# Closing the framework's context behind the first load, and a third direct block at the end

## The chip, the cores and the metric

The kernel runs on one core of one Trainium2 chip. The metric is device time of one launch in microseconds (us); lower is better. The core has TensorE (PE, with its weight loads as PEld), VectorE (DVE), ScalarE (ACT), GpSimd (POOL) and SyncE (SP, which here only issues transfers), and 16 DMA engines that all transfers share.

## What is computed

One decode step: a gated sum of an attention block over a long cache and an MLP block, for two rows `x` of 1024 numbers, all in float32.

```
g = sigmoid((x * gate_w).sum(-1, keepdims=True))
a = _A_ref(x, A_k_cache, A_v_cache, A_wq, A_wo)   # 32 query heads, 4 kv heads, 32768 keys
b = _B_ref(x, B_w1, B_w2, B_w3, B_w4)
return g * a + (1 - g) * b
...
x1 = x + hs            # S = 1: the shifted hs is 0, so w1 and w2 drop out
h2 = _gelu(_layernorm(x1, axis=-1) @ w3) @ w4
return x1 + h2
```

The cache and the weights, 331 MB, are read once. There are two rows of x and each number of the cache meets few numbers of the other operand, so nearly all of the work is the reading.

## The kernel before

All large inputs stream through two SBUF buffers of 128 rows by 16384 columns: `buf_a` takes `wq`, the keys `kt` and `wo`, and `buf_b` takes `w3`, `w4` and the values `vt`. A load fills one buffer (8 MB, 7 MB for `w3` and `w4`); the two alternate, 19 or 20 loads each. SP issues them in one queue; each but the first two waits for a count in `go`, which DVE raises when it has taken out the results that the buffer's matmuls left. TensorE goes through the rounds of `Fori(0, ROUNDS + 1)`: in each it waits for `landed_a`, multiplies the eight sets of `buf_a`, then the eight sets of `buf_b`. A set is four matmuls of 512 columns, one for each group `g`, and each group writes its own 32 PSUM rows. Round 0 has no sets: it does the small matmuls of the start (the transposed `x` from `xg`, the sums for the norm).

The last load is the second half of `w4`. It comes in five transfers, `PIECES = (6, 4, 2, 1, 1)` slabs of 1024 columns (a slab is 512 KB and one block of 128 rows of `w4`). The first ends sets 0 to 2 and has the semaphore `landed_b`; piece 1 ends sets 3 and 4, piece 2 set 5. The last `FIN = 2` slabs are not multiplied in sets: `block(c)` multiplies each straight into the result tile `acc`, in 16 short matmuls of 128 columns (eight, each in two passes). Between the two blocks TensorE adds what DVE has folded: at the end of set 3 DVE adds one bank of `ps_b` to `acc_sb`, at the end of set 5 the other in two halves (`masked`), and each half raises `folded`. Then DVE copies `acc` to `o_sb` and SP stores it.

The program's engine code stands between `tc.tile_critical(...)` and `tc.close()`. The framework's closing, which a later line calls, makes all engines meet twice (drains and semaphore instructions, profile line L578) while POOL clears the framework's semaphores. Behind it SP waits for the store.

Of the kernel before, what the change touches and what calls it, by code (L numbers as in the profile page):

```python
# [32 lines left out]
FIN = 2  # L33
EARLY = E * KT - FIN
PIECES = (6, 4, 2, 1, 1)
# [5 lines left out]
def kernel(  # L41
# [66 lines left out]
    store = nc.alloc_semaphore("store")  # L108

    with tc.tile_critical(sync_engine=POOL, no_gpsimd_drain=True):  # L110
        new = tc.alloc_semaphore
        landed = [new("landed_a"), new("landed_b")]
        pieces = [new(f"piece{i}") for i in range(1, len(PIECES))]
        folded, fin = new("folded"), new("fin")
        ready = [new("ready_a"), new("ready_b")]
        edge, pd, dvp, acp = new("edge"), new("pe_to_dve"), new("dve_to_pe"), new("act_to_pe")
        da, ad, dp, pc, go = (new(n) for n in (
            "dve_to_act", "act_to_dve", "dve_to_pool", "pool", "dve_to_sp"))
        v, s, t, g_, sy = nc.vector, nc.scalar, nc.tensor, nc.gpsimd, nc.sync

        def take(engine, sem, n=1):
            engine.wait_ge(sem, n).then_inc(sem, -n)  # L122

        def mm(o, lhsT, rhs, start=True, stop=True):
            return t.matmul(o, lhsT, rhs, start=start, stop=stop, skip_group_check=True)  # L125


        def sets(x, which, *events):
            for n4 in which:
                for g in range(G):  # L130
                    n, bank = n4 * G + g, n4 // 2 % 2
                    last = mm(ps[x][C * g:C * g + C, bank * 512:bank * 512 + 512],
                              wt[x][:, n * C:n * C + C], buf[x][:, n * 512:n * 512 + 512],
                              n4 in (0, 2), n4 in (3, 4, 5, 7))
                if n4 in events:
                    last.then_inc(pd, 1)

        def even(k):
            return t.If(k % 2 < 1)

        with t.Fori(0, ROUNDS + 1) as k:
            with t.If(k > 0):
                with t.If(k > 1):
                    sets(1, range(6, 8), 7)
                    with even(k):
                        take(t, dvp)
                        mm(sm[:, LP:LP + REP], ones, lsel).then_inc(pd, 1)
                        take(t, dvp)
                        for e in range(E):
                            last = mm(sm[:, OP + e * REP:OP + (e + 1) * REP],  # L150
                                      pv_t[:, e * P:(e + 1) * P], sel_all)
                        last.then_inc(pd, 1)
                take(t, landed[0], 16)
                take(t, ready[0])
                sets(0, range(8), 5, 7)
                with t.If(k < ROUNDS):
                    with even(k):
                        take(t, dvp)
                        t.transpose(sm[:1, MT:MT + P], m1, ident).then_inc(pd, 1)  # L159
                        take(t, dvp)  # L160
                        mm(sm[:, BP:BP + 1], mb, ones[:1, :1]).then_inc(pd, 1)
                    for q in range(2):
                        take(t, acp)
                        for j in range(4 * q, 4 * q + 4):
                            last = t.transpose(tr[:, j * P:(j + 1) * P], p[:, j * P:(j + 1) * P], ident)  # L165
                        last.then_inc(pd, 1)
                take(t, landed[1], 16)
                take(t, ready[1])
                sets(1, range(3))
                with t.If(k > ROUNDS - 1):  # L170
                    take(t, pieces[0], 16)
                sets(1, range(3, 5), 3)
                with t.If(k > ROUNDS - 1):
                    take(t, pieces[1], 16)
                sets(1, range(5, 6), 5)
            with t.Else():
                take(t, edge, 32)
                take(t, dvp)
                for w in range(4):
                    last = mm(tr[:, :48], spread[:, w * P:(w + 1) * P],  # L180
                              x16[:, w * 48:(w + 1) * 48], w == 0, w == 3)
                last.then_inc(pd, 1)
                take(t, dvp)
                for i in range(2):
                    last = mm(sm[:, SUMS + i * B:SUMS + i * B + B], ones, part[:, i * B:i * B + B])
                last.then_inc(pd, 1)
                take(t, dvp)
                mm(sm[:, VAR:VAR + B], ones, part2).then_inc(pd, 1)

        def eighths(lhsT, rhs, start=False, stop=False, halves=range(2)):  # L190

            for h in halves:
                for g in range(G):
                    w, col = lhsT(g), rhs(g, h)
                    first = HALF * (1 - h) + w[1]
                    last = mm(acc[C * g:C * g + C], w[0][:, first:first + C], col, start and h == 0, stop and h == 1)
            return last

        def block(c):
            def columns(g, h):  # L200
                col = (EARLY + c) * D + g * (D // G) + h * P
                return buf[1][:, col:col + P]
            return eighths(lambda g: (h_fin, c * C), columns, c == 0, c == FIN - 1)

        t.wait_ge(pieces[2], 16)
        block(0)
        for h in range(2):
            t.wait_ge(folded, h + 1)
            eighths(lambda g: (sel, g // 2 * C),
                    lambda g, h: acc_sb[:, (g % 2 * 2 + h) * P:(g % 2 * 2 + h + 1) * P], halves=[h])  # L210
        t.wait_ge(pieces[3], 16)
        block(1).then_inc(fin, 1)


        x_rows = xg.rearrange("(j q) k c -> j (q k c)", j=16)
        for lo, hi in ((0, 10), (10, 16)):
            s.dma_start(x16[lo:hi], x_rows[lo:hi]).then_inc(edge, 16)
        take(s, da)
        s.activation(gate, sm[:, SUMS:SUMS + B], AF.Sigmoid).then_inc(ad, 1)
        take(s, da)  # L220
        s.activation(dev, var, AF.Sqrt).then_inc(ad, 1)
        s.wait_ge(pc, 1)
        s.sem_inc(acp, 2)

        def turn(src, bank, func, to, *dims, **kw):

            return s.activation(at(p, to, *dims, (1, H)), at(src, bank * 512, (1, 2), (P, 4), (2, H)), func, **kw)  # L227

        for src in (qs, hs):
            take(s, da)  # L230
            for d in range(2):
                last = turn(src, 0, AF.Copy, d * H, (512, 2), (P, 4))
            last.then_inc(acp, 2)
        take(s, da)
        s.activation(bent, cube, AF.Tanh, scale=math.sqrt(2.0 / math.pi)).then_inc(ad, 1)
        with s.Fori(0, PAIRS):
            for i in range(NI):
                take(s, da)
                turn((s_sb, ps[0])[i // 2], i % 2, AF.Exp, i % 2 * 512, (256, 2), (H, 4), bias=bias, scale=scale,
                     accum_out=l4[:, i:i + 1]).then_inc(acp, 1)  # L240
            s.drain().then_inc(dp, 1)


        g_.memset(ident, 0.0)
        g_.memset(spread, 0.0)
        g_.drain()
        g_.affine_select(out=ident, in_=ident, compare_op=ALU.not_equal, fill=1.0, base=0,
                         pattern=[[-1, P]], channel_multiplier=1).then_inc(pc, 1)
        for tt in (wt_ab, zeros, buf[1][:, E * F * 2:]):
            g_.memset(tt, 0.0)  # L250
        g_.drain()
        for e in range(E):
            for kk in range(2):
                for tau, (lo, hi) in enumerate(halves):
                    g_.tensor_copy(
                        at(buf[1], E * F * 2 + (e * 2 + kk) * 512 + tau * 256 + kk * P + e, (2, H), rows=(lo, hi)),
                        at(ident, lo, (1, H), rows=(lo, hi)))
        g_.drain().then_inc(pc, 1)

        def x_to_queries(load):  # L260
            g_.tensor_copy(at(wt[0], 0, (256, 4), (34, 8), (1, B)),
                           at(xs, load * 12, (3, 4), (0, 8), (1, B))).then_inc(ready[0], 1)

        def queries(m):
            for tau, (lo, hi) in enumerate(halves):
                for u in range(2):
                    for e in range(E):
                        last = g_.tensor_copy(  # L268
# [5 lines left out]
        def heads(load):  # L274
# [4 lines left out]
            last.then_inc(ready[0], 1)  # L279

        take(g_, dp)
        x_to_queries(0)
        take(g_, dp)
        x_to_queries(1)
        take(g_, dp)
# [325 lines left out]
```

## Time and profile before

| | |
|---|---|
| time, median of 3 runs | 775.51 us (775.24 to 775.61) |
| profiled execution: time | 774.93 us |
| profiled execution: span, first to last instruction | 773.2 us |
| TensorE busy / weight loads / DVE | 407.5 us / 135.6 us / 160.9 us |
| read from HBM | 331.36 MB, 429 GB/s over the span |

The time is the launch's; the span is what the profiler sees between the first and the last instruction, and 1.7 us of the profiled execution lie around it. Matmuls of the four groups overlap and the busy time of TensorE is that of their union. In a row of the timeline "x24" counts instructions; a float32 matmul is two of them.

### The profile page before, as it was taken

The page shows a single profiled execution, that of the slowest core. Times are in us where ns is not written, and L with a number is a line of the kernel's source. Part 1 is how long each engine was busy: PE and PEld are TensorE (multiplying, and loading weights), DVE is VectorE, ACT ScalarE, POOL GpSimd, SP SyncE. Part 2 cuts the span into 40 slices and gives each one's busy share as a digit, 9 for nine tenths or more (in the row PEclk, how much of TensorE's full clock was granted, in tenths as well). Part 3 has the DMA queues.
Part 4 walks back from the last instruction along what each step waited for, and adds up shares of the span by engine and source line. Part 5 has one row for each costly group of instructions (what it writes and reads, how often), then busy time and mean ns, then how long its engine had stood idle before and what let it go on. Part 6 is the DMA issues. An engine that isn't in the chain of part 4 may idle for free. (4 is left out here: it accounts for less than half of the span.)

```text
span 773.2 us, 7166 instructions
## 1 busy us (share of the span) xinstructions
PE 407.5 (53%) x2845; PEld 135.6 (18%) x2845; DVE 160.9 (21%) x384; ACT 32.2 (4%) x74; POOL 22.5 (3%) x89
## 2 busy tenths in 40 slices
PE   1555465645554545545645554545445645554547
PEld 1111121211111111111211121111111211221112
DVE  4101030203120312031203120312031203120321
ACT  1000000100010001000100010001000100010000
POOL 4001000000000000000000000000000000000000
PEclk9977777677677777677677677777677677677779
DMA  9999999999999999999999999999999999999996
GB/s 381 434 434 434 440 429 434 434 434 434 434 434 434 434 434 434 434 434 431 434 434 434 434 434 434 434 434 434 434 434 434 434 434 434 434 434 434 434 417 293
DMA packets 6404, 331.41 MB, mean 429 GB/s; under 512 B 737, under 2 KB 769, under 8 KB 1025
## 3 DMA queue, kind: packets, MB, share of 16 engines
q1 hardware_dynamic: 6368, 331.36, 99.2%
q10 hardware_dynamic: 32, 0.01, 0.0%
q8 instruction: 1, 0.02, 0.0%
q14 instruction: 3, 0.02, 0.0%
HBM read 331.36 MB, written 0.01 MB: 429 GB/s over the span
## 5 line engine op out<-in xcount | busy, mean ns | idle before, releaser
L125 PE MATMUL ps_a<-buf_a,wt_ab 128*32 128x512 f32 x1280 | 183.0, 736 | 161.9 <-PEq L122 161.9
L125 PE MATMUL ps_b<-buf_b,wt_ab 128*32 128x512 f32 x1264 | 178.6, 727 | 125.3 <-PEq L122 125.3
L125 PEld LDWEIGHTS ps_a<-buf_a,wt_ab 128*32 128x32 f32 x1280 | 50.1, 132 | 285.8 <-issue 285.8
L125 PEld LDWEIGHTS ps_b<-buf_b,wt_ab 128*32 128x32 f32 x1264 | 49.1, 131 | 243.1 <-issue 243.1
L434 DVE TENSOR_REDUCE mx<-ps_a 128x1 f32<-128x512 f32 x34 | 23.5, 692 | 267.6 <-DVEq L122 250.5
L481 DVE COPY wt_ab<-tr 64x256 f32<-64x256 f32 x128 | 53.9, 421 | 18.3 <-DVEq L122 16.5
L227 ACT ACTIVATE zeros<-s_sb,bias 128x512 f32<-128x512 f32 x16 | 12.0, 750 | 539.7 <-ACTq L122 539.7
L165 PE MATMUL tr<-ident,zeros 128*128 128x128 f32 x152 | 25.7, 315 | 14.5 <-PEq L122 13.9
L385 DVE TENSOR_TENSOR pvs<-pvs,ps_b 128x512 f32<-128x512 f32 x8 | 5.5, 688 | 108.7 <-DVEq L122 108.7
L268 POOL COPY wt_ab<-q_all 64x64 f32 x64 | 12.3, 236 | 530.3 <-POOLq L122 529.6
L390 DVE COPY pvs<-ps_b 128x512 f32<-128x512 f32 x8 | 5.5, 691 | 86.3 <-DVEq L122 86.3
L165 PEld LDWEIGHTS tr<-ident,zeros 128*128 128x128 f32 x152 | 19.1, 159 | 24.5 <-issue 24.4
L125 PE MATMUL sm<-sel_all,zeros 128*128 128x8 f32 x40 | 7.1, 286 | 29.8 <-PEq L122 29.8
L125 PEld LDWEIGHTS sm<-sel_all,zeros 128*128 128x128 f32 x40 | 6.4, 230 | 30.3 <-issue 30.3
L227 ACT ACTIVATE zeros<-ps_a,bias 128x512 f32<-128x512 f32 x16 | 11.0, 687 | 14.9 <-ACTq L122 14.9
L438 DVE COPY s_sb<-ps_a 128x1024 f32<-128x1024 f32 x9 | 10.9, 1214 | 0.0
L159 PE MATMUL sm<-ident,m 128*1 128x128 f32 x9 | 2.4, 269 | 10.1 <-PEq L122 10.1
L125 PE MATMUL tr<-x,spread 16*128 16x48 f32 x8 | 1.9, 408 | 11.0 <-PEq L122 11.0
L125 PE MATMUL sm<-ones,mb 1*128 1x1 f32 x18 | 3.6, 264 | 6.9 <-PEq L122 6.9
L395 DVE SCALAR_TENSOR_TENSOR acc_sb<-ps_b,mask_g,acc_sb 128x512 f32<-128x512 f32 (+1 forms) x5 | 3.1, 642 | 13.6 <-PE ps_b L125 13.5
L522 DVE SCALAR_TENSOR_TENSOR tmp<-pvs,mss,tmp 128x128 f32<-128x128 f32 x16 | 5.6, 351 | 1.2
L392 DVE TENSOR_TENSOR pvs<-pvs,ps_b 128x512 f32<-128x512 f32 x8 | 5.5, 687 | 0.7
(98 smaller groups left out, 102.3 us busy)
## 6 DMA issues: line engine op xcount, KB each, us to landing
buf_b<-w SPq DMA_DIRECT2D x3, 7168.0 KB, 26.6
buf_b<-w SPq DMA_DIRECT2D x1, 3072.0 KB, 17.0
buf_b<-w SPq DMA_DIRECT2D x1, 2048.0 KB, 21.5
buf_b<-w SPq DMA_DIRECT2D x1, 1024.0 KB, 23.6
buf_b<-w SPq DMA_DIRECT2D x2, 512.0 KB, 24.7
buf_a<-kt SPq DMA_DIRECT2D x16, 28.3
buf_b<-vt SPq DMA_DIRECT2D x16, 28.4
buf_a<-wq SPq DMA_DIRECT2D x2, 24.5
```

What stands on the lines that cost most here:

```text
L125: return t.matmul(o, lhsT, rhs, start=start, stop=stop, skip_group_check=True)
L165: last = t.transpose(tr[:, j * P:(j + 1) * P], p[:, j * P:(j + 1) * P], ident)
L227: return s.activation(at(p, to, *dims, (1, H)), at(src, bank * 512, (1, 2), (P, 4), (2, H)), func, **kw)
L268: last = g_.tensor_copy(at(wt[0], e * 512 + u * P + u * 16 + tau * REP, (256, 2), (C, G), (1, REP), rows=(lo, hi)), q_all[lo:hi, bass.ds(m ...
L385: v.tensor_add(dst, dst, ps[x][:, :512]).then_inc(go, 1)
L390: v.tensor_copy(dst, ps[x][:, :512]).then_inc(go, 1)
L392: return v.tensor_add(dst, dst, ps[x][:, 512:])
L395: return v.scalar_tensor_tensor(at(acc_sb, *dims), at(src, *dims), mask_g, at(acc_sb, *dims), op0=ALU.mult, op1=ALU.add)
L434: last = v.reduce_max(out=mx[:, 2 * L + i:2 * L + i + 1], in_=ps[0][:, i * 512:(i + 1) * 512], axis=AX.X)
L438: v.tensor_copy(s_sb, ps[0]).then_inc(dp, 1)
L481: last = v.tensor_copy(at(wt[1], kp * P + q * H, (2 * P, 4), (REP, G), (C, 2), (1, REP), rows=dst), at(tr, q * 512 + tau * REP, (P, 4), (C ...
L522: v.scalar_tensor_tensor(tmp, pvs[:, ss * P:(ss + 1) * P], mss[:, ss:ss + 1], tmp, op0=ALU.mult, op1=ALU.add)
```

## The change

Six edits. Almost every line of the kernel is indented anew, since the `with` block now holds one line; the diff below leaves that out.

1. Only `load(0)` stands in `tile_critical`. `tc.close()` and `tc.compile()` follow at once, and all other code comes behind the closing, `load(1)` first. All semaphores come from `nc`.
2. Nothing follows the program's last instruction any more, except TensorE's own wait: it takes `store` where SP did.
3. `FIN` is 3 and `PIECES` (6, 5, 1, 1, 1). Piece 1 now ends sets 3, 4 and the first two groups of set 5; the other two groups of set 5, whose columns are the slab of `block(0)`, are left out in the last round.
4. The last piece but one (semaphore `pieces[2]`) goes out as four transfers of 96, 20, 10 and 2 rows (`SPLIT`).
5. In round 0 two small matmuls become one, and waits count up to 3 instead of taking 1 three times. In the tail the waits of TensorE for `folded` and of DVE for `pd` become takes (a semaphore instruction of its own).
6. POOL clears `wt_ab` and `zeros` in seven pieces instead of two.

```diff
-FIN = 2
+FIN = 3
-PIECES = (6, 4, 2, 1, 1)
+PIECES = (6, 5, 1, 1, 1)
+SPLIT = ((0, 96), (96, 116), (116, 126), (126, 128))
...
     with tc.tile_critical(sync_engine=POOL, no_gpsimd_drain=True):
+        load(0)
+
+    tc.close()
+    tc.compile()
+    load(1)
...
-                with t.If(k > ROUNDS - 1):
-                    take(t, pieces[1], 16)
-                sets(1, range(5, 6), 5)
+            sets(1, range(5, 6), 5, groups=range(2))
+            with t.If(k < ROUNDS):
+                sets(1, range(5, 6), groups=range(2, G))
...
-        t.wait_ge(pieces[2], 16)
+    take(t, pieces[1], 16)
         block(0)
         for h in range(2):
-            t.wait_ge(folded, h + 1)
+        take(t, folded)
             eighths(lambda g: (sel, g // 2 * C),
...
+    take(t, pieces[2], 16 * len(SPLIT))
+    block(1)
         t.wait_ge(pieces[3], 16)
-        block(1).then_inc(fin, 1)
+    block(2).then_inc(fin, 1)
+    t.sem_inc(pieces[3], -16)
+    take(t, store, 16)
...
-        for tt in (wt_ab, zeros, buf[1][:, E * F * 2:]):
+    for tt in (*wt, *parts, buf[1][:, E * F * 2:]):
...
         for sem, n in zip([landed[1], *pieces], PIECES):
-            sy.dma_start(buf[1][:, done * D:(done + n) * D],
-                         last_run[:, done * D:(done + n) * D]).then_inc(sem, 16)
+        for rows in SPLIT if sem is pieces[2] else [(0, P)]:
+            sy.dma_start(buf[1][rows[0]:rows[1], done * D:(done + n) * D],
+                         last_run[rows[0]:rows[1], done * D:(done + n) * D]).then_inc(sem, 16)
...
-    tc.close()
-    tc.compile()
-    nc.sync.wait_ge(store, 16).then_inc(store, -16)
+    sy.sem_inc(go, -len(loads))
```

The head of SP's program, before. The names in brackets are semaphores; those with 49 and "barrier" are the framework's.

```order
L607 UNCONDITIONAL_BRANCH [waits barrier_Pool_Activation_PE_DVE_SP_release]
L578 UNCONDITIONAL_BRANCH [waits Pool_sequencer_49]
L567 DMA buf_a<-wq 128x16384
L567 DMA buf_b<-w 128x14336
L567 DMA buf_a<-wq 128x16384 [waits dve_to_sp]
```

And now:

```order
L622 UNCONDITIONAL_BRANCH [waits barrier_Pool_Activation_PE_DVE_SP_release]
L143 UNCONDITIONAL_BRANCH [waits Pool_sequencer_49]
L137 DMA buf_a<-wq 128x16384
L139 UNCONDITIONAL_BRANCH
L143 UNCONDITIONAL_BRANCH [waits Pool_49]
L137 DMA buf_b<-w 128x14336 [waits SP_sequencer_49,Pool_sequencer_49,barrier_Pool_Activation_PE_DVE_SP_release]
L137 DMA buf_a<-wq 128x16384 [waits dve_to_sp]
```

The first load has kept its place; the closing, which stood behind the store, is now between it and the second load.

The end of TensorE's program before, from the wait for piece 1 on. Rows of round 0 and of the loop's end, which lie between, are left out of both pieces.

```order
L170 UNCONDITIONAL_BRANCH [waits piece1]
L125 MATMUL ps_b<-buf_b,wt_ab 32x512 x8
L173 COMPARE_AND_BRANCH
L173 UNCONDITIONAL_BRANCH [waits piece2]
L125 MATMUL ps_b<-buf_b,wt_ab 32x512 x4
...
L125 MATMUL acc<-buf_b,zeros 32x128 [waits piece3]
L125 MATMUL acc<-buf_b,zeros 32x128 x7
...
L125 MATMUL acc<-buf_b,zeros 32x128 [waits piece4]
L125 MATMUL acc<-buf_b,zeros 32x128 x7
```

And now:

```order
L195 UNCONDITIONAL_BRANCH [waits piece1]
L150 MATMUL ps_b<-buf_b,wt_ab 32x512 x10
L199 COMPARE_AND_BRANCH
L150 MATMUL ps_b<-buf_b,wt_ab 32x512 x2
...
L150 MATMUL acc<-buf_b,zeros 32x128 [waits piece2]
L150 MATMUL acc<-buf_b,zeros 32x128 x7
...
L150 MATMUL acc<-buf_b,zeros 32x128 [waits piece3]
L150 MATMUL acc<-buf_b,zeros 32x128 x7
L150 MATMUL acc<-buf_b,zeros 32x128 [waits piece4]
L150 MATMUL acc<-buf_b,zeros 32x128 x7
```

Ten matmuls (sets 3, 4 and half of 5) now stand behind one wait, where there were eight and then four behind two; behind the folded part, which is left out of both, two blocks follow instead of one. The two matmuls behind the compare are skipped in the last round.

## Rows read from the trace of the kernel before

**Rows 1.** The page, 40 slices of the span: DMA busy tenths, and GB/s.
```profile
DMA  9999999999999999999999999999999999999996
GB/s 381 434 434 434 440 429 434 434 434 434 434 434 434 434 434 434 434 434 431 434 434 434 434 434 434 434 434 434 434 434 434 434 434 434 434 434 434 434 417 293
```

**Rows 2.** Timeline of the end: start, length, instructions, idle before and its releaser.
```profile
742.67 2.23 SPq L572 DMA_DIRECT2D buf_b<-w  x5
...
761.49 2.76 PE L125 MATMUL ps_b<-buf_b,wt_ab 128*32 128x512 f32 x24
...
764.69 1.92 PE L125 MATMUL ps_b<-buf_b,wt_ab 128*32 128x512 f32 x16 [0.44 <-PEq L122]
...
767.21 1.06 PE L125 MATMUL ps_b<-buf_b,wt_ab 128*32 128x512 f32 x8 [0.60 <-PEq L122]
768.33 0.88 DVE L395 SCALAR_TENSOR_TENSOR acc_sb<-ps_b,mask_g,acc_sb 128x256 f32<-128x256 f32 x2 [1.77 <-PE ps_b L125]
...
768.36 0.65 PE L125 MATMUL acc<-buf_b,zeros 128*32 128x128 f32 x16
...
769.56 0.65 PE L125 MATMUL acc<-buf_b,zeros 128*32 128x128 f32 x16
770.27 0.29 DVE L547 COPY o_sb<-acc 128x128 f32<-128x128 f32 x1 [1.06 <-PE acc L125]
770.59 0.55 SPq L576 DMA_DIRECT2D out<-o_sb  x1
```

**Rows 3.** Stretches of the end: busy times, then granted clock, DMA share, GB/s.
```profile
767.10:768.30 1.20, 1.06 (x8) 0.19 (x8) 0.00 (x0) 0.00 (x0) 0.00 (x0) 1.00 0.30 120
768.30:770.30 2.00, 1.84 (x48) 1.07 (x48) 0.91 (x3) 0.00 (x0) 0.00 (x0) 1.00 0.03 10
```

**Rows 4.** Issues: the store, KB, us from issue to landing.
```profile
out<-o_sb SPq DMA_DIRECT2D x1, 8.0 KB, 1.7
```

**Rows 5.** Line L578, the closing: durations in ns, first and last start.
```profile
L578 SPq EVENT_SEMAPHORE  x4: 17/22/28, 771.6 to 773.1; - x4
...
L578 PEldq EVENT_SEMAPHORE  x2: 51/51/51, 772.0 to 773.1; - x2
```

**Rows 6.** Timeline of the start.
```profile
0.89 0.38 SPq L567 DMA_DIRECT2D buf_a<-wq  x1
0.90 0.93 ACTq L217 DMA_DIRECT2D x<-xg  x2
...
1.33 0.43 SPq L567 DMA_DIRECT2D buf_b<-w  x1
...
10.96 1.91 PE L125 MATMUL tr<-x,spread 16*128 16x48 f32 x8 [10.96 <-PEq L122]
```

**Rows 7.** Timeline of the first two loads' use and the third load's issue.
```profile
24.52 9.59 PE L125 MATMUL ps_a<-buf_a,wt_ab 128*32 128x512 f32 x64 [6.98 <-PEq L122]
...
34.89 0.33 SPq L567 DMA_DIRECT2D buf_a<-wq  x1
...
41.45 9.65 PE L125 MATMUL ps_b<-buf_b,wt_ab 128*32 128x512 f32 x64 [6.32 <-PEq L122]
```

**Rows 8.** Three stretches round a pause of TensorE, columns as in rows 3.
```profile
69.90:72.30 2.40, 0.00 (x0) 0.00 (x0) 0.86 (x2) 1.21 (x2) 0.00 (x0) 1.00 0.88 382
72.30:73.40 1.10, 1.06 (x8) 0.86 (x8) 0.00 (x0) 0.00 (x0) 0.00 (x0) 1.00 1.68 730
...
74.00:77.70 3.70, 0.00 (x0) 0.00 (x0) 0.46 (x3) 0.00 (x0) 2.48 (x9) 0.50 0.98 423
```

**Rows 9.** Weight loads, four per pass of a set, in the first burst of matmuls.
```profile
25.34 0.23 PEld L125 LDWEIGHTS ps_a<-buf_a,wt_ab 128*32 128x32 f32 x4 [0.63 <-issue]
26.20 0.23 PEld L125 LDWEIGHTS ps_a<-buf_a,wt_ab 128*32 128x32 f32 x4 [0.63 <-issue]
...
31.34 0.13 PEld L125 LDWEIGHTS ps_a<-buf_a,wt_ab 128*32 128x32 f32 x4 [0.29 <-issue]
31.77 0.13 PEld L125 LDWEIGHTS ps_a<-buf_a,wt_ab 128*32 128x32 f32 x4 [0.29 <-issue]
```

More of the change, by code (lines that the diff above doesn't have):

```diff
@@ new lines @@
+    new = nc.alloc_semaphore
+    landed = [new("landed_a"), new("landed_b")]
+    pieces = [new(f"piece{i}") for i in range(1, len(PIECES))]
+    folded, fin = new("folded"), new("fin")
+    ready = [new("ready_a"), new("ready_b")]
+    edge, pd, dvp, acp = new("edge"), new("pe_to_dve"), new("dve_to_pe"), new("act_to_pe")
+    da, ad, dp, pc, go, store = (new(n) for n in (
+        "dve_to_act", "act_to_dve", "dve_to_pool", "pool", "dve_to_sp", "store"))
+    v, s, t, g_, sy = nc.vector, nc.scalar, nc.tensor, nc.gpsimd, nc.sync
@@ new lines, in load, with take, mm, sets @@
+    def load(j):
+        x, src = loads[j]
+        sy.dma_start(buf[x][:, :src.shape[1]], src).then_inc(landed[x], 16)
+    with tc.tile_critical(sync_engine=POOL, no_gpsimd_drain=True):
+        load(0)
+    tc.close()
+    tc.compile()
+    load(1)
+    def take(engine, sem, n=1):
+        engine.wait_ge(sem, n).then_inc(sem, -n)
+    def mm(o, lhsT, rhs, start=True, stop=True):
+        return t.matmul(o, lhsT, rhs, start=start, stop=stop, skip_group_check=True)
+    def sets(x, which, *events, groups=range(G)):
+        for n4 in which:
+            for g in groups:
+                n, bank = n4 * G + g, n4 // 2 % 2
+                last = mm(ps[x][C * g:C * g + C, bank * 512:bank * 512 + 512],
+                          wt[x][:, n * C:n * C + C], buf[x][:, n * 512:n * 512 + 512],
+                          n4 in (0, 2), n4 in (3, 4, 5, 7))
+            if n4 in events:
+                last.then_inc(pd, 1)
@@ new lines, in eighths, with block, columns @@
+    def eighths(lhsT, rhs, start=False, stop=False, halves=range(2)):
+        for h in halves:
+            for g in range(G):
+                w, col = lhsT(g), rhs(g, h)
+                first = HALF * (1 - h) + w[1]
+                last = mm(acc[C * g:C * g + C], w[0][:, first:first + C], col, start and h == 0, stop and h == 1)
+        return last
+    def block(c):
+        def columns(g, h):
+            col = (EARLY + c) * D + g * (D // G) + h * P
+            return buf[1][:, col:col + P]
+        return eighths(lambda g: (h_fin, c * C), columns, c == 0, c == FIN - 1)
@@ new lines, in queries @@
+    def queries(m):
+        for tau, (lo, hi) in enumerate(halves):
+            for u in range(2):
+                for e in range(E):
+                    last = g_.tensor_copy(
+                        at(wt[0], e * 512 + u * P + u * 16 + tau * REP, (256, 2), (C, G), (1, REP), rows=(lo, hi)),
+                        q_all[lo:hi, bass.ds(m * (E * REP) + e * REP, REP)]
+                        .rearrange("p (a c h) -> p a c h", a=1, c=1).to_broadcast([H, 2, G, REP]))
+        last.then_inc(ready[0], 1)
@@ new lines, in heads @@
+    def heads(load):
+        for tau, (lo, hi) in enumerate(halves):
+            last = g_.tensor_copy(
+                at(wt[0], 0, (2 * C, E * REP), (C, 2), (1, B), rows=(lo, hi)),
+                at(o_all, (2 * load + tau) * B * E * REP, (1, E * REP), (0, 2), (E * REP, B), rows=(lo, hi)))
+        last.then_inc(ready[0], 1)
+    take(g_, dp)
+    x_to_queries(0)
+    take(g_, dp)
+    x_to_queries(1)
+    take(g_, dp)
+    g_.memset(wt[0], 0.0)
+    g_.drain()
+    with g_.Fori(0, PAIRS) as m:
+        queries(m)
@@ L281 @@
         take(g_, dp)
[L282 removed]
+        g_.sem_inc(ready[0], 1)
         take(g_, dp)
[L284 to L303 removed]
@@ new lines @@
+    got()
+    for tau, (lo, hi) in enumerate(halves):
+        last = v.tensor_copy(at(xs, 0, (12, 2), (6, E), (1, 6), rows=(lo, hi)),
+                             at(tr, 6 * tau, (12, 2), (24, E), (1, 6), rows=(lo, hi)))
+    last.then_inc(dp, 1)
+    wait_order()
+    v.tensor_mul(v3(xw), x_kb, at(xs, B, (3, KD), (0, B)))
+    wait_order()
+    v.tensor_reduce(part[:, 0:B], vb(xw), axis=AX.X, op=ALU.add)
+    v.tensor_reduce(part[:, B:2 * B], x_bk, axis=AX.X, op=ALU.add).then_inc(dvp, 1)
+    got()
@@ new lines, with scores @@
+    wait_order()
+    for b in range(B):
+        last = v.tensor_copy(at(q_all, b * E * REP, (REP, E), (B * E * REP, HKV), (4, 2), (1, 4)),
+                             at(qraw, b, (64, E), (4, HKV), (2, 2), (16, 4)))
+    last.then_inc(dp, 1)
+    got(3)
+    more(hs, 1).then_inc(da, 1)
+    wait_order()
+    v.tensor_scalar_mul(acc_sb, hs, mask_r)
+    def scores(L):
+        for i in range(2):
+            got()
+            last = v.reduce_max(out=mx[:, 2 * L + i:2 * L + i + 1], in_=ps[0][:, i * 512:(i + 1) * 512], axis=AX.X)
+        last.then_inc(go, 1)
@@ new lines, with hidden @@
+    wait_order()
+    v.tensor_mul(cube, hid, inner)
+    wait_order()
+    for b in range(B):
+        v.tensor_scalar_mul(at(h_all, b, (B, E), (4 * E * B, KT), (E * B, 4)),
+                            at(cube, 6 + b, (96, E), (2, KT), (24, 4)), rest[:, b:b + 1])
+    wait_order()
+    def hidden(load):
+        for tau, (lo, hi) in enumerate(halves):
+            last = v.tensor_copy(
+                at(wt[1], 0, (KT * 2 * C, E), (2 * C, KT), (C, 2), (1, B), rows=(lo, hi)),
+                at(h_all, (2 * load + tau) * KT * E * B, (B, E), (E * B, KT), (0, 2), (1, B), rows=(lo, hi)))
+        last.then_inc(ready[1], 1)
@@ L343, with got @@
+    def got(n=1):
+        take(v, pd, n)
+    with v.Fori(0, PAIRS) as m:
+        scores(1)
+        wait_order()
+        v.reduce_max(out=m1, in_=mx, axis=AX.X).then_inc(dvp, 1)
         got()
-        for tau, (lo, hi) in enumerate(halves):
-            last = v.tensor_copy(at(xs, 0, (12, 2), (6, E), (1, 6), rows=(lo, hi)),
-                                 at(tr, 6 * tau, (12, 2), (24, E), (1, 6), rows=(lo, hi)))
-        last.then_inc(dp, 1)
+        v.reduce_max(out=m8, in_=sm[:1, MT:MT + P].rearrange("p (s h) -> p h s", h=REP), axis=AX.X)
@@ L429 @@
[L429 to L438 removed]
+        v.tensor_copy(bias, sm[:, BP:BP + 1]).then_inc(da, 2)
+        turned(0, da, None)
+        turned(1, da, ready[1])
+        got(3)
@@ new lines @@
+    v.drain().then_inc(dp, 1)
+    hidden(1)
+    masked_sums(s_sb)
+    wait_order()
+    got(2)
+    masked_sums(ps[0])
+    wait_order()
+    got()
+    masked(ps[1][:, 512:], 0, (1, 512))
+    wait_order()
+    got()
+    for h in range(2):
+        masked(ps[1], h * P, (2 * P, 2), (1, P)).then_inc(folded, 1)
+    v.wait_ge(fin, 1)
+    v.tensor_copy(o_sb, acc).then_inc(go, 1)
+    v.sem_inc(fin, -1)
+    for j in range(2, len(loads)):
+        sy.wait_ge(go, j - 1)
+        load(j)
+    last_run = tiles(w4, 1)
```

640 lines of the change are left out of this document (260 added, 380 removed).

## Prediction

> **What bounds the kernel now.** I read the slices of the page first. The DMA engines are at nine tenths or more in 39 of 40 slices, at 434 GB/s in nearly all of them [rows 1]. So the time is a short start, 331 MB at that rate, and a tail. No edit changes the bytes, and work in the middle of the stream, such as splitting set 5 in two, lies beside it. Only three places can move the time: the start, if a later start of the engines makes the stream run dry; the stretch from the arrival of the last pieces to the store; and what follows the store.
>
> The timeline of the end comes next [rows 2]. TensorE starts on piece 1 at 764.69, on piece 2 at 767.21, on the two blocks at 768.36 and 769.56; DVE folds from 768.33, copies the result at 770.27, and SP issues the store at 770.59. From piece 2 on, the chain of compute and the arrival of the last slab are nearly level: DVE's two halves end at 769.21, and the last block starts 0.35 us later. The DMA engines are mostly done by then, at a share of 0.30 and then 0.03 in the last two stretches [rows 3]: what still arrives comes from one or two of the 16 engines, which are late.
>
> Last, what follows the store. It lands 1.7 us after its issue [rows 4], at 772.29. The span ends at 773.2. The 0.9 us between are the closing: its semaphore instructions run on SP from 771.6 to 773.1 [rows 5], and only then can SP see the store.
>
> **The end of the program.** The closing goes away there, and TensorE waits for the store itself. Its semaphore instruction takes 0.05 us [rows 5]; with as much for its start the program ends 0.1 us after the landing instead of 0.9 us. That is -0.8. At best TensorE sees the landing at once, -0.9; if some other step at the end takes as long as half the closing did, -0.4.
>
> **The tail.** The pieces after the first now hold 5, 1, 1 and 1 slabs.
>
> *When piece 1 is there.* Between pieces 1 and 2 of before lay two slabs and 2.52 us, 1.26 us a slab [rows 2]. One slab more than before puts TensorE's start at 764.69 + 1.26 = 765.95. The neighbouring spacings, 768.36 - 767.21 = 1.15 and 1.20 for the last, make it 0.1 us less at most.
>
> *How long the sets take.* Four matmuls of a set run side by side: eight instructions take 1.06 us, sixteen 1.92, twenty-four 2.76 [rows 2], so a further set costs 0.85. Half of set 5 has two groups instead of four, but each group still runs through its 512 columns, so I take the full 0.85; if half the matmuls took half the time it would be 0.43. The three sets end at 765.95 + 2.76 = 768.71. Before, set 5 ended at 768.27 and DVE started 0.06 us later; now DVE starts at 768.77, 0.44 us later than the 768.33 of before. This is the heart of the forecast: the last slab that goes through a set arrives one slab earlier, but three sets, not one, wait for it.
>
> *From the fold to the copy.* Before, the copy came 1.94 us after DVE's start (770.27 - 768.33). One more block now stands behind the fold. A block streams 2 x 128 columns per group and pass, half of a set's 512, so it costs 0.43 when it follows another; alone it took 0.65 [rows 2]. The copy starts at 768.77 + 1.94 + 0.43 = 771.14, which is 0.87 later. Block 0 is not in this sum: it needs piece 2, the 12th slab, which by the same spacing is there at 767.21, and runs in the time in which TensorE waits for DVE anyway. The two takes of `folded` are semaphore instructions of some 0.05 us, within the bounds. For the block the bounds are 0.2 (its start hidden) and 0.65.
>
> *The last four transfers.* SP issues five in 2.23 us by 744.9 [rows 2], so three more end at some 746.2, twenty us ahead of need. The last slab is needed at 771.14 - 0.71 = 770.43 (the last block started 0.71 before the copy). It was there at 769.56 before, 0.87 us earlier. So moving the last arrival by a few tenths either way changes nothing in this sum.
>
> **The start.** The first load keeps its place at 0.89. Behind it comes the closing, at its price at the end of before, from the store's issue at 771.14 to 773.2, some 2.1 us. The second load is issued at about 3.3 instead of 1.33 [rows 6], with the first load, which is in use from 24.5 on, still in flight for 20 us: hidden. ACT's transfers of `x`, POOL's clearing (now seven pieces) and everything of DVE start 2.2 us later. The small `x` waits behind the big load: TensorE's first matmul on it came at 10.96, nine us after ACT was done issuing at 1.83 [rows 6]. Now both its transfers are issued into a stream already running, so I take 2.2 us at least and, if they wait a full round longer (nine us once more is not in question, half of it is), 6.7 at most. The cover is 6.98 us: so long does TensorE sit idle before the first load's matmuls at 24.52 [rows 7]. Behind it is a second one: the third load is issued at 34.89 and the second is in use only from 41.45, so the stream has a further 4 to 6 us. The start costs nothing; if both covers were gone, each us late would be a us of time.
>
> **The sum.** -0.8 + 0.87 + 0 = +0.1 us, span 773.3 for 773.2, and with the 1.7 us around it 775.0 for the profiled 774.93. The median of the runs shown is 775.51, 0.6 above the profiled run, so the forecast is **775.6**. The bounds of its terms: -0.9 to -0.4 for the end; for the tail 0.87 less 0.1, 0.42 and 0.23, or more by 0.1 and 0.22. That is -0.8 to +0.8, 774.7 to 776.3. A measurement of this kernel can tell about 0.2%, 1.55 us, from no change.
>
> **The rivals.**
> *The clock of TensorE falls in the new pause (slower).* [...] At the low level a pass takes 0.85 us (25.34 to 26.20) instead of 0.43 [rows 9]. Then the three sets cost 2.6 us more, 778.2; if the clock falls in the middle of them about half. It decides when one of the sets still runs at the low level. [...]
>
> *The tail stays bound by the last slab's arrival (faster).* If TensorE's sets, folds and blocks are shorter than worked out, the late DMA engine decides as it may now, and the copy comes 0.71 us after the last arrival. With the arrival unmoved the tail is as before and the end's 0.8 remains: 774.7. If the split takes rows off the late engine, it arrives earlier; the bounds for that are nothing and the whole spacing of a slab, 1.2 us. The slab's bytes are the same and no row shows which engine is late, so I take nothing, with 773.5 as the far end. Rows 2 speak against it, with 0.87 us between need and arrival. [...]
>
> *The end does not get shorter.* The launch's time counts more than the span. If what comes behind it takes as long whoever waits, only the tail's 0.87 is left: 776.4.
>
> *The start runs dry.* If `x` waits for the whole first load, the first matmuls start some 13 us late instead of at most 7, and the third load is issued past the second's end: about +2 to +3, 778.
>
> **How the numbers follow.** The forecast's own case 0.62; arrival-bound tail 0.15; clock 0.12, of which a quarter stays under 777.06; end not shorter 0.07; start 0.04. Within 0.2% are the first, most of the second, the fourth and a quarter of the clock: 0.82. Faster by more than 0.2% needs 1.55 us, more than the arrival-bound tail gives unless the late engine is much less late in this program: 0.05. Slower 0.13. For 8 in 10 the range takes in the first two and the end not shorter, with part of the clock: 774.2 to 777.2.
>
> **What would show it.** Right: the second load issued near 3.3, with no thin slice of DMA in the first 60 us; one burst of 20 instructions on piece 1, starting near 765.95 and ending near 768.7 at a clock of 1.00; DVE's halves near 768.8, two blocks back to back behind them, the copy near 771.1 and the end of the span 2.1 us behind it instead of 2.9. Wrong: a clock of 0.50 behind the pause; half of set 5 in half the time; a wait between the last two blocks (then the arrival binds); matmuls of the first load later than 24.5.

## The result and the profile after

The changed kernel takes 776.69 us (median of 17 runs, 775.66 to 778.63) against 775.19 for the kernel before beside it (774.70 to 775.97). The ratio is 1.0018, with a 95% interval of 1.0011 to 1.0026: slower by 1.5 us, within the 0.2%, inside the range, and 1.4 us worse than the +0.1 of the sum. The interval lies above 1: the loss is small, but it is one. Its profiled execution has a span of 775.0 us and a time of 776.88.

The start first, in the timeline of the changed kernel (start, length, instructions; columns as in [rows 6]):

```profile
0.89 0.40 SPq L137 DMA_DIRECT2D buf_a<-wq  x1
2.31 0.33 SPq L137 DMA_DIRECT2D buf_b<-w  x1
...
2.31 0.94 ACTq L245 DMA_DIRECT2D x<-xg  x2
...
15.58 1.91 PE L150 MATMUL tr<-x,spread 16*128 16x48 f32 x8 [15.58 <-PEq L147]
...
24.38 9.06 PE L150 MATMUL ps_a<-buf_a,wt_ab 128*32 128x512 f32 x64 [2.77 <-PEq L147]
...
34.22 0.33 SPq L137 DMA_DIRECT2D buf_a<-wq  x1
```

The closing now delays the second load to 2.31 (1.33 in [rows 6]) and `x` by 4.6 us (15.58 for 10.96). TensorE still starts on the first load at 24.38 and the third load is issued at 34.22, no later than in [rows 7] (24.52 and 34.89). Of the cover of 6.98 us 2.77 are left; the start costs nothing.

Now the end, in the timeline and then in stretches of 1 us (busy times of PE, PEld, DVE, ACT, POOL, then granted clock, DMA share, GB/s):

```profile
760.84 2.76 PE L150 MATMUL ps_b<-buf_b,wt_ab 128*32 128x512 f32 x24
...
766.17 3.79 PE L150 MATMUL ps_b<-buf_b,wt_ab 128*32 128x512 f32 x18 [2.57 <-PEq L147]
...
769.78 0.61 PE L150 MATMUL ps_b<-buf_b,wt_ab 128*32 128x512 f32 x2
...
770.53 0.88 DVE L424 SCALAR_TENSOR_TENSOR acc_sb<-ps_b,mask_g,acc_sb 128x256 f32<-128x256 f32 x2 [1.51 <-DVEq L147]
...
771.78 1.08 PE L150 MATMUL acc<-buf_b,zeros 128*32 128x128 f32 x32
772.92 0.29 DVE L576 COPY o_sb<-acc 128x128 f32<-128x128 f32 x1 [1.50 <-PE acc L150]
773.24 0.55 SPq L593 DMA_DIRECT2D out<-o_sb  x1
```

```profile
764.00:765.00 1.00, 0.00 (x0) 0.00 (x0) 0.00 (x0) 0.00 (x0) 0.00 (x0) 1.00 0.95 381
765.00:766.00 1.00, 0.00 (x0) 0.00 (x0) 0.00 (x0) 0.00 (x0) 0.00 (x0) 0.86 1.08 274
766.00:767.00 1.00, 0.83 (x5) 0.23 (x9) 0.00 (x0) 0.00 (x0) 0.00 (x0) 0.50 1.07 197
767.00:768.00 1.00, 1.00 (x12) 0.37 (x8) 0.00 (x0) 0.00 (x0) 0.00 (x0) 0.50 1.04 180
768.00:769.00 1.00, 1.00 (x12) 0.29 (x6) 0.73 (x1) 0.00 (x0) 0.00 (x0) 0.50 0.96 229
769.00:770.00 1.00, 1.00 (x12) 0.29 (x8) 0.03 (x1) 0.00 (x0) 0.00 (x0) 0.94 0.43 107
770.00:771.00 1.00, 0.82 (x14) 0.34 (x10) 0.47 (x2) 0.00 (x0) 0.00 (x0) 1.00 0.11 45
```

Stretches of the kernel before, from 765 on:

```profile
765.00:766.00 1.00, 1.00 (x13) 0.31 (x8) 0.19 (x1) 0.00 (x0) 0.00 (x0) 1.00 1.06 426
766.00:767.00 1.00, 0.61 (x8) 0.00 (x0) 0.56 (x1) 0.00 (x0) 0.00 (x0) 1.00 0.99 397
767.00:768.00 1.00, 0.79 (x8) 0.19 (x8) 0.00 (x0) 0.00 (x0) 0.00 (x0) 1.00 0.43 168
768.00:769.00 1.00, 0.92 (x24) 0.51 (x24) 0.67 (x2) 0.00 (x0) 0.00 (x0) 1.00 0.09 37
```

The reader is to see two things, neither in the sum. The granted clock falls to 0.50 in the pause ahead of piece 1, which is 2.57 us long and not 1.7 (from 764.25, where the sets before it ended in [rows 2], to the 765.95 that was worked out), and stays there for most of the sets: 4.22 us (766.17 to 770.39) instead of 2.76. And the DMA engines, as busy as before (share 1.07 and 1.04), move 197 and 180 GB/s instead of 397 to 426: in the DMA records of the two traces a packet of 4 KB takes some 0.36 us there and 0.16 in the kernel before (medians). The last traffic, some 40 GB/s, falls in 770 to 771 and not in 768 to 769. The copy starts at 772.92, not 771.14. From there to the span's end it is 2.1 us, as worked out, instead of 2.9.

Clock and arrival are both late by about the same, so this one profile can't say which of them costs the 1.5 us. Theory 1 is the clock, theory 2 the four transfers, and the sum without either is +0.1.

### The profile page after: what moved, and what is told of

Same layout as the page of the kernel before. It is cut to its first block, busy times and chain, and to the rows that moved or that the text cites. A ratio compares the mean times of both kernels' runs of the same rounds, so it can differ in the third digit from the quotient of the medians.

```text
span 775.0 us, 7191 instructions
## 1 busy us (share of the span) xinstructions
PE 410.3 (53%) x2855; PEld 137.1 (18%) x2855; DVE 161.0 (21%) x384; ACT 32.2 (4%) x74; POOL 22.6 (3%) x94
## 5 line engine op out<-in xcount | busy, mean ns | idle before, releaser
L150 PE MATMUL ps_b<-buf_b,wt_ab 128*32 128x512 f32 x1260 | 181.6, 739 | 126.4 <-PEq L147 126.4
```

## The experiments

"Before" is the kernel before, run beside each; its median is 774.83 to 774.89, and 775.19 in the first row. The span of every execution beside e1 to e13 is known too; its median for before is 772.9 to 773.0. The time outside the span is 1.7 to 1.9 us in most executions of most kernels.

| kernel | time, median (n) | ratio to before, 95% | span, median (range) |
|---|---|---|---|
| changed kernel | 776.69 (17) | 1.0018 (1.0011 to 1.0026) | 774.9 (773.8 to 775.5) |
| the same once more (e9) | 776.37 (11) | 1.0020 (1.0011 to 1.0029) | 774.5 (773.9 to 775.6) |
| matmuls in the pause (e1) | 776.06 (11) | 1.0012 (1.0003 to 1.0021) | 774.2 (773.8 to 774.8) |
| no split (e4) | 775.66 (11) | 1.0009 (1.0000 to 1.0018) | 773.1 (772.9 to 775.1) |
| both (e5) | 776.04 (11) | 1.0015 (1.0006 to 1.0024) | 773.4 (772.9 to 773.9) |
| end alone (e2) | 774.15 (11) | 0.9990 (0.9981 to 0.9999) | 772.3 (772.1 to 772.4) |
| end + split (e6) | 776.86 (11) | 1.0020 (1.0011 to 1.0029) | 775.0 (773.7 to 775.5) |
| end + two halves (e7) | 778.00 (5) | 1.0038 (1.0024 to 1.0052) | 776.0 (775.0 to 776.2) |
| end + even and odd rows (e8) | 774.27 (11) | 0.9991 (0.9982 to 1.0000) | 772.4 (772.1 to 772.6) |
| end, SP waits (e10) | 773.83 (11) | 0.9989 (0.9980 to 0.9998) | 772.3 (772.0 to 773.6) |
| end + more pieces (e11) | 774.27 (11) | 0.9993 (0.9984 to 1.0001) | 772.4 (772.1 to 772.7) |
| end + long pause (e12) | 777.89 (7) | 1.0032 (1.0020 to 1.0044) | 775.6 (773.8 to 776.8) |
| the same, matmuls in it (e13) | 775.84 (11) | 1.0014 (1.0005 to 1.0023) | 774.0 (773.8 to 774.4) |

**e1, matmuls in the pause.**

```
             with t.If(k > ROUNDS - 1):
+                for i in range(2):
+                    for g in range(G):
+                        mm(tr[C * g:C * g + C, i * 512:i * 512 + 512],
+                           wt[1][:, g * C:g * C + C], buf[1][:, g * 512:g * 512 + 512])
                 take(t, pieces[0], 16)
```

> The changed kernel, plus eight matmuls of 512 columns that TensorE runs after the last round's sets 1 and 2, ahead of its wait for piece 1, on data that has landed; nobody reads their result. They fill 1.7 us of the pause of 2.57 us. Theory 1 (the loss is the clock that fell in the pause): the granted clock stays at 1.00 to the end, the three sets on piece 1 take 2.8 us instead of 4.2, and what then ends last is the arrival of the split slab and the last one, still at 770.7 and 771.7; the copy starts near 772.4 instead of 772.9, and the time is 0.5 us under the changed kernel's, some 0.9 over the kernel before. Rival (the pause's clock does not matter, the arrival alone sets the end): the clock may stay up, the time is that of the changed kernel, 1.4 to 1.5 over before. Had the split no effect on the arrival, the whole 1.5 us of the clock would come back: 0.1 over before.

The copy starts at 772.33 and the span is 774.4. The clock is 1.00 in every stretch of the end, and the sets take 2.77 us. Then the arrival binds, as the releaser of the last block's weights says (a stretch and the timeline of e1):

```profile
767.00:768.00 1.00, 1.00 (x14) 0.39 (x8) 0.67 (x1) 0.00 (x0) 0.00 (x0) 1.00 1.03 180
```

```profile
766.09 2.77 PE L150 MATMUL ps_b<-buf_b,wt_ab 128*32 128x512 f32 x20
...
771.61 0.38 PEld L150 LDWEIGHTS acc<-buf_b,zeros 128*32 128x32 f32 x16 [0.26 <-DMA buf_b<-w]
772.33 0.29 DVE L580 COPY o_sb<-acc 128x128 f32<-128x128 f32 x1 [2.44 <-PE acc L150]
```

In time it is 1.2 over before, more than the 0.9 expected, and its interval overlaps that of the changed kernel.

**e4, no split.**

```
-SPLIT = ((0, 96), (96, 116), (116, 126), (126, 128))
+SPLIT = ((0, 128),)
```

> The changed kernel with the last slab but one in one transfer of 128 rows instead of four. Theory 2 (the transfers of 96, 20, 10 and 2 rows slow the stream): the GB/s of the last 6 us are again at 400 and the last slab lands near 769.5 instead of 771.7. If the arrival set the changed kernel's end, the time falls by up to 1.5 us, to 0.1 over before. If theory 1 holds (the clock falls in the pause in front of piece 1, and the slow sets alone set the end), the time stays where the changed kernel's is, 1.4 over before, with the copy near 772.9 and a clock of 0.50 on the sets, though the slab is there 2 us earlier.

Half of this was wrong. The stream is back at 414 GB/s in 766 to 767 and empty by 769, but the clock didn't fall either: piece 1 is there earlier (765.70), TensorE happens to end the first piece's sets later (764.93 for 763.60), and the pause is 0.77 us. So the tail ran as forecast, with the copy at 771.00 for 771.14 (a stretch and the timeline of e4):

```profile
766.00:767.00 1.00, 1.00 (x13) 0.33 (x9) 0.07 (x1) 0.00 (x0) 0.00 (x0) 1.00 1.03 414
```

```profile
765.70 2.34 PE L150 MATMUL ps_b<-buf_b,wt_ab 128*32 128x512 f32 x18 [0.76 <-PEq L147]
...
768.62 0.88 DVE L424 SCALAR_TENSOR_TENSOR acc_sb<-ps_b,mask_g,acc_sb 128x256 f32<-128x256 f32 x2 [0.93 <-DVEq L147]
...
769.86 1.08 PE L150 MATMUL acc<-buf_b,zeros 128*32 128x128 f32 x32
771.00 0.29 DVE L576 COPY o_sb<-acc 128x128 f32<-128x128 f32 x1 [1.50 <-PE acc L150]
```

Its span, 773.1, is 0.2 over before. Its time is 0.8 over, because the time outside the span is 2.4 us or more in 5 of 11 executions. One execution in 11 had a span of 775.1; none of that was traced.

**e5, both** (the edits of e1 and e4).

> The changed kernel with both: the eight matmuls in the pause and the last slab but one in one transfer. If clock and split are the two causes and each hides the other, both run costs are gone: clock 1.00, last landing near 769.5, copy near 771.1, time 0.1 over before, 1.3 to 1.5 under the changed kernel. If one of the two is no cause, this kernel is as fast as the better of the two single ones. If a third thing costs the time (three sets on piece 1, the longer start), it stays at 1 us or more over before.

Clock 1.00, copy at 771.46, span 773.4. The extra matmuls end only when piece 1 is already there and cost 0.3 to 0.5 of this. The time didn't follow the span: outside it lie 2.4 us or more in 9 of 11 executions. So the time is 1.2 over before with both suspects gone, which is the case that the expectation gave to a third cause. The two that it named, the three sets and the longer start, would show in the span, which is only 0.4 to 0.5 over before; most of the 1.2 lies outside it. In the profiled execution an instruction fetch begins at 775.2, 1.6 us behind the last instruction (the trace's DMA queues from 775 on):

```profile
DMA packets 1, 0.02 MB, mean 4 GB/s; under 512 B 0, under 2 KB 0, under 8 KB 0
## 3 DMA queue, kind: packets, MB, share of 16 engines
q8 instruction: 1, 0.02, 1.5%
```

**e2, the end alone** (the changed kernel with `FIN = 2`, `PIECES = (6, 4, 2, 1, 1)` in whole transfers, all of set 5).

> The changed kernel with the tail of the kernel before: pieces of 6, 4, 2, 1 and 1 slabs, no split, two blocks. Start and end are those of the change. Theory (the end's closing is worth 0.8 us in the launch's time, the start is hidden): 0.8 under before, 774.4, with the span's end 2.1 us behind the copy instead of 2.9. Rival (what comes behind the span takes as long whoever waits): the span is 0.8 shorter and the time that of before, 775.2. A second rival, the later start costs: over 775.2.

As expected, with 0.7 us for 0.8: copy at 770.08, the span's end 2.1 behind it (timeline of e2).

```profile
766.90 1.07 PE L149 MATMUL ps_b<-buf_b,wt_ab 128*32 128x512 f32 x8 [0.57 <-PEq L146]
...
770.08 0.29 DVE L573 COPY o_sb<-acc 128x128 f32<-128x128 f32 x1 [1.07 <-PE acc L149]
```

So in launch time the changed end is a gain, and the tail gives it back three times over. e4 against e2 is the tail in whole transfers: span 773.1 for 772.3, +0.8, where the forecast had +0.87.

**e6, the split alone**, in the end-alone kernel.

```
+SPLIT = (slice(0, 96), slice(96, 116), slice(116, 126), slice(126, 128))
...
-    take(t, pieces[2], 16)
+    take(t, pieces[2], 16 * len(SPLIT))
...
-        for rows in [(0, P)]:
+        for rows in SPLIT if sem is pieces[2] else [slice(0, P)]:
...
```

> The kernel of the end alone (closing moved, TensorE waits for the store, tail of the kernel before) plus one thing of the change's tail: the last slab but one comes in the four transfers of 96, 20, 10 and 2 rows. Theory 2 (the four transfers slow the stream): packets of 4 KB take 250 to 400 ns instead of 160 in the last stretches, the last slab lands near 771.5 instead of 769.4, the last block starts behind it, the copy moves from 770.1 to about 772.2 and the time from 774.15 to some 776.2, 1.4 over before. Rival (my forecast's: where rows land makes no difference to the last arrival): the time of the end alone, 0.7 under before. If only the longer tail of the changed kernel made the split dear, it costs a few tenths here.

2.7 us dearer than the end alone, more than theory 2 alone had it. The piece that is issued ahead of the split comes 1.6 us later too (768.52 for 766.90), which opens a pause of 2.00 us. The clock is still 1.00 in the pause and behind it; it falls to 0.50 between 770 and 771, where the blocks begin, and they pay for it (timeline, then three stretches of e6):

```profile
768.52 1.07 PE L150 MATMUL ps_b<-buf_b,wt_ab 128*32 128x512 f32 x8 [2.00 <-PEq L147]
```

```profile
767.00:768.00 1.00, 0.00 (x0) 0.00 (x0) 0.00 (x0) 0.00 (x0) 0.00 (x0) 1.00 0.99 188
...
770.00:771.00 1.00, 0.73 (x16) 0.76 (x20) 0.63 (x2) 0.00 (x0) 0.00 (x0) 0.68 0.10 41
771.00:772.00 1.00, 1.00 (x28) 1.00 (x23) 0.00 (x0) 0.00 (x0) 0.00 (x0) 0.50 0.00 0
```

Its spans fall into two groups, 773.7 to 774.0 (five executions) and 775.0 to 775.5 (six, the profiled one among them). The lower group is 1.5 over e2's 772.3, where theory 2 by itself had 2.05. That the clock stayed up in that group is not shown, since none of it was traced.

**e7, two halves.** As e6, with `SPLIT = (slice(0, 64), slice(64, 128))`.

> As the kernel of the end alone, with the last slab but one in two transfers, rows 0 to 63 and 64 to 127: 4 rows for each of 16 engines in both. [...] If it is the number of transfers, or the engines left without a row in the small ones, two transfers of 64 cost next to nothing: 0.7 under before. [...]

**e8, even and odd rows.** As e6, with `SPLIT = (slice(0, 128, 2), slice(1, 128, 2))`.

> As the kernel of the halves, with the even rows in one transfer and the odd ones in the other: the same 4 rows for each of 16 engines, the same number of transfers and packets, but each spread over all 128 partitions. If the place of the rows decides, this costs nothing: 4 KB packets at 160 ns, 0.7 under before. If the number of transfers or their size decides, it is as slow as the halves are.

The two are alike in number of transfers, in bytes and in rows, and in both the DMA engines are about fully busy. Three stretches and a timeline row of e7:

```profile
765.00:766.00 1.00, 1.00 (x16) 0.31 (x8) 0.10 (x1) 0.00 (x0) 0.00 (x0) 1.00 1.18 209
766.00:767.00 1.00, 0.59 (x8) 0.00 (x0) 0.66 (x1) 0.00 (x0) 0.00 (x0) 1.00 0.95 180
...
771.00:772.00 1.00, 1.00 (x20) 1.00 (x24) 0.42 (x2) 0.00 (x0) 0.00 (x0) 0.50 0.03 12
```

```profile
769.31 1.07 PE L150 MATMUL ps_b<-buf_b,wt_ab 128*32 128x512 f32 x8 [2.72 <-PEq L147]
```

and of e8:

```profile
765.00:766.00 1.00, 1.00 (x16) 0.31 (x12) 0.00 (x0) 0.00 (x0) 0.00 (x0) 1.00 1.00 401
766.00:767.00 1.00, 0.81 (x8) 0.00 (x0) 0.75 (x1) 0.00 (x0) 0.00 (x0) 1.00 1.00 401
```

```profile
767.12 1.06 PE L150 MATMUL ps_b<-buf_b,wt_ab 128*32 128x512 f32 x8 [0.31 <-PEq L147]
```

Half the rate in one, the full rate in the other, 778.0 against 774.27. It is not how many transfers there are, but which rows go together in one. The rows of `w4` that a transfer reads in HBM change with the rows of SBUF that it fills, and no run changes one alone. The whole transfers read the same rows at 397 to 426 GB/s, so their spacing in HBM isn't it; that reading one half of them at a time costs something is not ruled out by a run. e7 cost 3.85 us over the end alone, for the same two reasons as e6: the piece ahead comes at 769.31, and the clock falls to 0.50 behind a pause of 2.72 us.

**e9, the changed kernel once more.**

> The changed kernel once more, for a second profile and for times beside the three others. Its first profile had a pause of 2.57 us before piece 1 and a clock of 0.50 behind it. Theory 1: the pause is 1.5 us or more in every execution, the clock falls again, and the time is 1.4 over before. Rival: the pause changes from one execution to the next with the landing of the last loads; where it is short the clock stays at 1.00, the slow arrival of the split alone is left, and the span is near 773.8, the shortest of the changed kernel's so far, instead of 775.

The profile is of one of the long executions: a pause of 2.29 us, the clock at 0.50 from 767 to 770, the sets from 766.46 on in 4.5 us, span 775.6. Over the 28 executions of the two runs the span goes from 773.8 to 775.6; 13 lie above 774.8, the longest of e1, whose pause was filled. That fits a clock that falls in about half of the executions, and it would explain why this kernel scatters; an execution of the short kind was not profiled, so it isn't shown. The sets in the profile (timeline of e9):

```profile
766.46 4.04 PE L150 MATMUL ps_b<-buf_b,wt_ab 128*32 128x512 f32 x18 [2.29 <-PEq L147]
...
770.30 0.63 PE L150 MATMUL ps_b<-buf_b,wt_ab 128*32 128x512 f32 x2
```

**e10, SP waits for the store** in place of TensorE, in the end-alone kernel.

```
     t.sem_inc(pieces[3], -16)
-    take(t, store, 16)
...
     sy.sem_inc(go, -len(loads))
+    take(sy, store, 16)
```

> The kernel of the end alone, with SP instead of TensorE waiting for the store at the end. Theory (the 0.7 us of the end alone come from the closing that no longer stands between landing and end): the same as the end alone, 774.15, 0.7 under before, the end 0.1 us behind the landing. Rival (it matters that TensorE waits, because SP is busy or sees the store later): 0.2 to 0.7 us more.

The span is that of the end alone, 772.3, but the time is 773.83: 1.0 under before where e2 was 0.7 under it. Outside the span lie 1.54 us (median; 1.52 to 1.61 in ten of eleven executions) instead of 1.87, and 1.81 to 1.87 in e11, where TensorE waits too. The rival was wrong in the other direction: it matters who waits, and TensorE is the dearer one. The 0.3 us are clear outside the span; in time the intervals of e10 and e2 overlap. Three of e10's spans are 0.8 to 1.3 us longer than the others; none of these was traced.

**e11, more pieces**: `PIECES = (6, 4, 1, 1, 1, 1)` with the three direct blocks, and half of set 5 waits for its own slab.

> The changed kernel's three direct blocks, but pieces of 6, 4, 1, 1, 1 and 1 slabs in whole transfers, so that the sets 3 and 4 start as early as in the kernel before and only half of set 5 waits for the next slab. TensorE's pauses are short, its folds end near 768.8, and the last block waits for the last slab at 769.3: copy near 770.0, 774.1, as the end alone or 0.1 under it. If the last arrival is not the floor of this tail, up to 0.5 less; if the third block costs its 0.43 on the path, 774.6.

774.27, the same as e2 within the measurement: with three blocks the tail is no shorter than with two. Nor is it longer. e11 is e4 with its piece of five slabs cut into four and one, and its span is 0.7 shorter (772.4 for 773.1), so nearly all that the tail costs in e4 comes from that piece. In e11 the last block's weights are released by the DMA at 769.46: the last arrival is the floor there.

**e12, a long pause without a split**: the end-alone kernel with `PIECES = (6, 6, 1, 1)` and no wait ahead of set 5.

> The kernel of the end alone with 6, 6, 1 and 1 slabs: no split, but TensorE waits for one piece of six slabs, from about 764.2 to 767.0, 2.8 us, and then runs the sets 3, 4 and 5 on end. It measures the clock's price by itself. Theory 1: the granted clock falls to 0.50 in or right behind the pause, the three sets take 4.2 us or more instead of 2.76, the copy starts at 773.3 or later, time 777.4 or more. Rival (the clock stays up over a pause, as it did over 2.5 us in mid-stream): sets end at 769.8, copy at 771.9, 775.95.

**e13, the same with twelve matmuls in the pause** (as in e1, in three rounds of four instead of two).

> As the kernel of the long pause, with twelve matmuls of 512 columns in the pause on data that has landed, some 2.55 us; nobody reads their result. Theory 1: clock 1.00 to the end, sets on the piece end at 769.8, copy at 771.9, 775.95, 1.4 us or more under the kernel of the long pause. Rival (the clock plays no part): the same time as that kernel.

Timeline and two stretches of e12:

```profile
767.22 5.35 PE L149 MATMUL ps_b<-buf_b,wt_ab 128*32 128x512 f32 x24 [3.35 <-PEq L146]
```

```profile
766.00:767.00 1.00, 0.00 (x0) 0.00 (x0) 0.00 (x0) 0.00 (x0) 0.00 (x0) 0.50 0.97 389
...
768.00:769.00 1.00, 1.00 (x12) 0.33 (x8) 0.00 (x0) 0.00 (x0) 0.00 (x0) 0.50 0.10 41
```

and of e13:

```profile
766.98 2.78 PE L149 MATMUL ps_b<-buf_b,wt_ab 128*32 128x512 f32 x24 [0.78 <-PEq L146]
```

```profile
768.00:769.00 1.00, 1.00 (x15) 0.31 (x8) 0.75 (x1) 0.00 (x0) 0.00 (x0) 1.00 0.08 33
```

Twelve matmuls more, and the kernel is 2.05 us faster in the median. The clock's price is 5.35 - 2.78 = 2.6 us for three sets, and by the spans five of e12's seven executions paid more than half of it or all (775.5 to 776.8; the other two, 773.8 and 774.2, are like e13).

## Why the prediction was right, and where it failed

**The number.** 776.69 lies in the range of 774.2 to 777.2, but not in the -0.8 to +0.8 us that the bounds of the sum's own terms allow. It is inside because the range was drawn wider, to take in rivals. And +1.5 us stays just under the 0.2% (1.55 us) that stood for no clear change: that part came true by luck, with two costs in it that the sum had at nothing.

**The end: right.** -0.8 was forecast; copy to end went from 2.9 to 2.1 us, and alone it is worth 0.7 of launch time. "The end does not get shorter" asked for the time of before in e2. e2's interval ends just under 1; the three other kernels with this end and no slow transfer in the tail (e8, e10, e11) lie 0.6 to 1.0 under before as well, which speaks against it.

**The start: right in its result, off in its size.** The second load went out at 2.31 and not at about 3.3: behind the first issue, which ends at 1.29, the closing took 1.0 us and not 2.1. The price at the end of before, from the store's issue on, was the wrong one to carry over. `x` came 4.6 us later, between the bounds. All of it was hidden.

**The tail as work: right.** Three sets in 2.8 us, the third block behind the fold, +0.87: in whole transfers it measured +0.8 in the span (e4 against e2). The half of set 5 does take the time of a whole one (20 instructions in 2.77 us in e1, 24 in 2.76 before).

**The last four transfers: the step that failed.** "Moving the last arrival by a few tenths either way changes nothing in this sum" took the split as a matter of tenths. It moved the last arrival by 2 us or more, past the 0.87 of slack: the last block's data is there at 771.61 in e1, and at 769.56 at the latest before. With the clock up, split against no split is 774.2 against 773.1 in the span (e1 against e4): +1.1. Against e5, which has e1's matmuls as well, it is +0.8. I had weighed that the split takes rows off the late engine, and found that no row shows which one that is; I did not ask which rows a transfer holds. e7 and e8 show that what decided it is which rows go together: 180 to 209 GB/s for halves and 401 for even and odd rows. Why neighbouring rows come at half the rate no run shows, and that the changed kernel's 180 to 230 GB/s have the same cause is argued from e7, not measured.

**The clock: a rival given too little.** It had 0.12, on the strength of one row [rows 8] where the clock was still at 1.00 behind a pause of 2.5 us. That the two paces of [rows 9] are two levels of the clock was my reading: the profile gives the granted clock as 1.00 at both. The changed kernel does show two: a pass of a set takes 0.85 us at a clock of 0.50 (767.00 to 767.85, from one group of weight loads to the next) and 0.43 at 1.00 (761.27 to 761.70). The price of 2.6 us for three sets is what e12 against e13 measured. What I missed is that the pause's length is not fixed: it hangs on a late piece 1 (the split slows it by some 0.4 to 0.8 us: 766.17, 766.46 and 766.09 with it in the changed kernel, e9 and e1, for 765.70 in e4) and on when TensorE ends the sets before (763.60 to 764.93 in these profiles). In the changed kernel the clock costs some 0.7 to 1.4 us where it seems to have fallen (the long spans, 774.9 to 775.6, for e1's 774.2) and 0.3 to 0.7 in the median (774.5 and 774.9 for 774.2). It is less than the 1.5 us that the sets lose (4.22 for 2.76), because the late arrival hides part of it.

In the span the steps are -0.7 for the end, +0.8 for the tail, +1.1 for the split and 0.3 to 0.7 for the clock: +1.5 to +1.9, against +1.5 to +2.0 measured. That they add up proves nothing, since each is the difference of two neighbouring medians; what shows the causes is the traces and the runs that take one thing alone (e6 to e8 for the split, e12 and e13 for the clock). In time the same steps don't close. Taking away the clock alone gave some 0.3 us back, the split alone 0.7, both together 0.3 (e1, e4 and e5; 1.2, 0.8 and 1.2 over before instead of 1.5, with intervals that overlap).

**What stays open.** Without the split (e4, e5) the span is within 0.5 us of before, yet the time is 0.8 to 1.2 over, since the time outside the span grows in many executions. The late instruction fetch of e5 fits that, and e9's profiled execution, where one begins 2.2 us behind the span, has 3.0 us outside it; in two other profiled executions it begins before the last instruction (e11 at 769.9, e1 at 772.1), and they have the usual 1.86 and 1.89 us outside. No run was made that moves that fetch, so it isn't shown to be the cause, and the launch's time of e4 and e5 stays unexplained.

The lowest time here is that of e10, the changed end alone with SP waiting: 773.83 us, 0.11% under before.

## What to carry to other kernels

When a transfer is cut by rows, ask which rows, not only how many: cut by columns, as the pieces of whole slabs are (397 to 426 GB/s in the kernel before), or take every second row (401 in e8), because blocks of neighbouring rows halved the rate here (180 to 209 in e7), of their own transfers and of the ones beside them. A piece that arrives later in exchange for fewer pieces lengthens a pause of TensorE, and a pause can have a price of its own (2.6 us for three sets behind one of 3.35 us, e12 against e13): read the granted clock of the stretch behind it in several executions before trusting one row. And when two things are late by the same amount, take each away alone and then both, since either alone showed little here (0.3 us in time for the clock, 0.7 for the split).

## What the runs showed of the hardware that was not expected

- The choice of rows decided the rate: 180 to 209 GB/s with a slab in two blocks of 64 neighbouring rows (e7), 401 with 64 rows two apart (e8), with the engines about equally busy (shares 0.95 to 1.18 and 1.00). The whole transfer issued ahead of them was slowed too: its data is used 1.6 us later in e6 and 2.4 in e7 (768.52 and 769.31 for 766.90 in e2).
- The last wait of the program cost more on TensorE (e2) than on SP (e10): 1.87 and 1.54 us outside the span, 774.15 and 773.83 us in time, at the same span.
- Two profiled executions of the changed kernel have pauses of 2.57 and 2.29 us ahead of the last sets, with TensorE done before them at 763.60 and 764.16. By the spans the granted clock seems to fall in some executions of a program and not in others; only executions of the long kind were traced.
- An instruction fetch of 16 KB can begin after the last instruction, and the time outside the span, 1.7 to 1.9 us in most executions, was 2.1, 2.3 and 3.0 in the three profiled executions that show one there (e6, e5, e9).
